# Moving the split of the next unit's values, the maxima ahead of it and the row scales in a fused attention and feed-forward kernel

## The chip, the cores and the metric

The kernel runs on one core of one Trainium2 chip. The metric is the device time of one execution in microseconds. The kernel before takes 1301.77 us (median of three runs, 1301.55 to 1302.38).

## What is computed

Eight batches with eight heads each, 576 tokens, head dimension 64. The scores of a head are thresholded: a row keeps only the scores within `tau` of its maximum, takes their softmax, and multiplies it with the values. The heads of a batch are put side by side (512 columns), and the 4608 rows go through a feed-forward layer with 2048 hidden columns and softplus between its two products.

```python
scores = scale * np.matmul(q, k.transpose(0, 1, 3, 2))
thresh = np.max(scores, axis=-1, keepdims=True) - tau
scores = np.where(scores >= thresh, scores, -1000000000.0)
attn = np.exp(scores - np.max(scores, axis=-1, keepdims=True))
attn = attn / (np.sum(attn, axis=-1, keepdims=True) + 1e-09)
x = np.matmul(attn, v)                       # then heads side by side
h = x @ w_in
out = (np.maximum(h, 0.0) + np.log1p(np.exp(-np.abs(h)))) @ w_out
```

## The kernel before

**Units, tiles and steps.** A unit is a pair of heads of one batch: 32 units. Each has nine tiles of 128 rows of scores by 576 columns (tile 4 holds the last 64 rows of both heads). The outer loop (L1020) runs over all 288 tiles; its pass for tile `t` of unit `u` is called step `t` of unit `u` here. A step does the parts of several tiles at once, in an order that a string of letters gives (`PAT`, L35: `RemhlTfpSxfvwp`). In the step of tile g these are:

- R: `row_max` (L493) of tile g+2, on DVE, written to `negm`.
- e: `exps` (L499) of tile g+2, on ACT: the exponentials `e_all`, and a small operation that makes the threshold `thr`.
- m: `mask` (L504) of tile g+1, on DVE: compares the scores in PSUM with `thr` and multiplies `e_all`, summing the row into `sums`. It is the last reader of the tile's scores.
- h: `weights_hi` (L569) of tile g+1, on POOL: the upper 16-bit half `h` of the weights.
- l: `weights_lo` (L578) of tile g, on DVE: the lower half, also called `h` in the profile. It needs POOL's half of the same tile, made a step earlier.
- T: `weights_T` (L583) of tile g-1: a transposing DMA of both halves, on SP's queue, to `eT`.
- f (twice): a share of the feed-forward products on PE (`h` L725, `o` L789). Their share of each step is set by hand (`Q9`, L40). Softplus (`st`, on ACT) and its halves (`g`, on POOL) and the additions (`acc`, on DVE) follow.
- p (twice): a point, at which deferred work becomes due (`defer`, L888: n points later).
- S: `scores` (L475) of tile g+3, on PE. There are two PSUM buffers for scores, so those of tile g+3 take the one that the mask of tile g+1 has freed.
- x: `extras` (L948): everything that comes once a unit.

**The order on the engines.** From step 36 on, every operation on DVE, ACT and POOL is tied behind the one that was issued before it on the same engine (class `Queue`, L149), so these three run in the order of the program text. PE and SP have no such tie: their order is fixed when the program is built, by the order of the text and by what is expected to be ready. [...] What the three tied engines run is recorded under line 156.

**What comes once a unit.** In `extras` of unit `u`: products of weights and values (`values`, L595, steps 7 and 8 of the same unit and 2 and 3 of the next, nine matmuls `pv` each, then an ACT copy and a DVE addition to `xp`); splitting and transposing keys and queries of the next unit (steps 0 to 8, L936); loads of keys and queries of the unit after (steps 7 and 8). The values of unit `u+1` are handled in unit `u`: `load_v` (L366, three DMAs to `vn`, one buffer) at step 0, `top_v` (L376) at step 3, `split_v` (L393) at step 7. `top_v` takes the maxima of `vn` on DVE (`vtop`); two points later PE spreads them over the partitions, one point later DVE makes the power of two `v_scale` of them. `split_v` scales `vn` on ACT in place, one point later POOL writes its 16-bit halves to `vt` (two buffers), and four points later `turn_v` (L399) copies them with swapped partitions by two DMAs. This concerns units 5 to 31; the first five (`whole`, L341) use unsplit weights and values.

**Row scales.** `row_scales` (L616) adds 1e-9 to the row sums, multiplies by `v_scale` and takes the reciprocal, two DVE operations on 128 by 9 numbers (`rs`). `extras` calls it at step 8. At step 1 of the next unit (`RT`, L39) `row_scales_T` has PE transpose them; ACT, a DMA out and three DMAs back spread them to `R`, and seven points later POOL multiplies `xp` by `R`. The result, halved by `split_x` (L698), is the input of the feed-forward layer, which works in chunks: six of its main chunks (512 rows, one batch) begin at steps 43, 80, 116, 152, 188 and 224 (L910), so one takes four units.

```python
  if t == RT and prev:
      row_scales_T(prev)
  if t == 8:
      row_scales(cur)
...
  else:
      times = ((s.i - 1, 0), (s.i - 1, 3), (s.i - 1, 7))
  for at_, f in zip(times, (load_v, top_v, split_v)):
      plan.setdefault(at_, []).append(lambda f=f, s=s: f(s))
```

Of the kernel before, what the change touches and what calls it, by code (L numbers as in the profile page):

```python
# [38 lines left out]
RT = 1  # L39
# [26 lines left out]
def tile_kernel(ctx: ExitStack, tc: tile.TileContext, q, k, v, tau, w_in, w_out, out):  # L66
# [270 lines left out]
    for b in range(B):  # L337
        for hp in range(NPAIR):
            s = Unit()
# [243 lines left out]
    def weights_T(s, t):  # L583
        if t in (0, M):
            j = int(t == M)
            s.eT[j] = apool.tile([P, 9, S], F16, tag="eT", bufs=2, name=f"eT_{s.i}_{j}")
        h = s.e16.pop(t)
        if t == M:
            for j in range(2):
                nc.sync.dma_start_transpose(s.eT[j][:, :, SM:S], h[j * SR:(j + 1) * SR])  # L590
            return
        j, c = divmod(t, NC + 1)
        nc.sync.dma_start_transpose(s.eT[j][:, :, c * P:(c + 1) * P], h)

    def values(s, g):  # L595
        if g == 0:
            s.xp = apool.tile([P, S], F32, tag="xp", bufs=NX, name=f"xp_{s.i}")
        j, x0 = g // 2, g % 2 * HS
        o = ps_g.tile([P, 512], F32, tag="g", name=f"pv_{s.i}_{g}")

        steps = [(v_slot(j, NC), NC)]
        for c in range(NC):
            steps += [(v_slot(j, c), c), (10 + v_slot(j, c), 2 * NC - c)]
        for n, (a, b) in enumerate(steps):
            nc.tensor.matmul(o[:, 0:HS], s.vt[:, a, :], s.eT[j][:, b, x0:x0 + HS], start=(n == 0), stop=(n == 2 * NC))  # L605
        defer(1, lambda: values_out(s, g, o))
# [9 lines left out]
    def row_scales(s):  # L616
        s.rs = apool.tile([P, 9], F32, tag="rs", name=f"rs_{s.i}")
        if s.whole:
            vec.tensor_scalar(out=s.rs, in0=s.sums, scalar1=1e-9, scalar2=None, op0=ALU.add)
        else:  # L620
            vec.tensor_scalar(out=s.rs, in0=s.sums, scalar1=1e-9, scalar2=v_scale[:, s.i:s.i + 1],
                              op0=ALU.add, op1=ALU.mult)
        vec.reciprocal(s.rs, s.rs)

    def row_scales_T(s):
        ps = ps_g.tile([P, 512], F32, tag="g", name=f"rT_{s.i}")
        nc.tensor.transpose(ps[0:9, 0:P], s.rs, ident)
        defer(1, lambda: row_scales_out(s, ps))
# [307 lines left out]
    def pre(s, first_):  # L936

        def a():
            split_k(s)
        def b():  # L940
            split_q(s, 0)
            qkT(s, 0, 0)
        def d():
            split_q(s, 1)
        return [a, b, lambda: qkT(s, 0, 2), lambda: qkT(s, 0, 1), d, lambda: qkT(s, 1, 0), lambda: qkT(s, 1, 1),
                lambda: qkT(s, 1, 2)]

    def extras(i, t):  # L948

        cur = units[i]  # L950
        nxt = units[i + 1] if i + 1 < len(units) else None
        prev = units[i - 1] if i else None
        for s, t_ in ((prev, t + 9), (cur, t)):
            if s and t_ in (VW if s.whole else VO):
                (whole_values if s.whole else values)(s, (VW if s.whole else VO).index(t_))
        if t == RT and prev:
            row_scales_T(prev)
        if t == 8:
            row_scales(cur)
        if nxt:  # L960
            if t == 0:
                cur.nxt = pre(nxt, False)
            for n, f in enumerate(cur.nxt):
                if ST[n] == t:
                    f()
        for f in plan.pop((i, t), ()):
            f()
        for at_, f in zip(LD, (load_k, load_q)):
            if t == at_ and i + 2 < len(units):
                f(units[i + 2])  # L970

    plan = {}
    for s in units:
        if s.i == 0:
            times = ((0, -1), (0, 0))
        elif s.i == 1:
            times = ((0, -1), (0, 4))
        elif s.whole:
            times = ((s.i - 1, 4), (s.i - 1, 7))
        else:  # L980
            times = ((s.i - 1, 0), (s.i - 1, 3), (s.i - 1, 7))
        for at_, f in zip(times, (load_v, top_v, split_v)):
            plan.setdefault(at_, []).append(lambda f=f, s=s: f(s))

# [35 lines left out]
    for g, (cur, t) in enumerate(tiles):  # L1020
# [7 lines left out]
        for step in PAT:  # L1028
# [6 lines left out]
            elif step == "h" and nxt and not nxt[0].whole:  # L1035
                weights_hi(*nxt)
            elif step == "l" and not cur.whole:
                weights_lo(cur, t)
            elif step == "R" and ahead:
                row_max(*ahead)  # L1040
            elif step == "e" and ahead:
                exps(*ahead)
            elif step == "m" and nxt:
                mask(*nxt)
            elif step == "f":
                upto += quota / PAT.count("f")
                while done < upto:
                    done += next(ffn)
            elif step == "x":
                extras(cur.i, t)  # L1050
            elif step == "S" and g + 3 < NS:
                scores(*tiles[g + 3])
            elif step == "v":
                slow_products()
            elif step == "w":
                while prep and prep[0][0] <= g:
                    _, f, a = prep.pop(0)
                    f(*a)
            elif step == "p":
                point()  # L1060

    last = units[-1]
    weights_T(*tiles[-1])
    rest = {15: lambda: row_scales_T(last), 21: lambda: values(last, 2), 24: lambda: values(last, 3)}
    for n, _ in enumerate(ffn):
# [35 lines left out]
```

## Time and profile before

| | us |
|---|---|
| median of three runs | 1301.77 |
| the profiled execution, its own time | 1300.2 |
| its span, first to last instruction | 1298.4 |
| PE busy | 1231.9 |
| DVE busy | 931.2 |
| POOL busy | 912.7 |
| ACT busy | 906.2 |

A row of a group or of the timeline names the start (timeline only), the busy time, the engine, the line, the operation, what it writes and reads (`out<-in`), the shape and the count; in brackets stands the time that the engine was idle before it and what ended that. PEld is TensorE's loading of weights, which overlaps its products. A row of waits gives who waited for whom, the total in us, the number of times and the longest. In the timeline, instructions of one kind that follow one another are merged into one row. In the window that the next section uses, 665 to 674 us, the masks (`e_all<-s,thr,e_all`) of 666.04, 668.93 and 672.97 us belong to step 7 and step 8 of unit 18 and step 0 of unit 19; the steps of units 8 to 24 take 573 us, from 296 to 869 us.

### The profile page before, as it was taken

The numbers are of one execution on the slowest core, as the hardware profiler recorded it, in microseconds if no ns is written. First come the engines' busy times: TensorE is split into PE (matmuls) and PEld (weight loads), VectorE is DVE, ScalarE is ACT, GpSimd is POOL, SyncE is SP. The second block draws the span as 40 slices with busy tenths as digits, with TensorE's granted clock in tenths as the row PEclk, the third lists the DMA queues.
The fourth block names the chain that finished last, engine by engine and source line by source line (L and its number), as shares of the span: only waits on it lengthen the run. The fifth ranks groups of instructions, "written<-read, shape, count | busy, mean of one in ns | idle before, by whom it ended". The sixth has DMA issues, their size and how long they took to land.

```text
span 1298.4 us, 21573 instructions
## 1 busy us (share of the span) xinstructions
PE 1231.9 (95%) x7045; PEld 741.9 (57%) x7045; DVE 931.2 (72%) x1738; ACT 906.2 (70%) x1715; POOL 912.7 (70%) x986
## 2 busy tenths in 40 slices
PE   6988987898999999999999999999999999999998
PEld 5655544454566566556555655665657755554455
DVE  6878888989878887788778977786677666640111
ACT  5877887877777777777777787778676767744321
POOL 2577788978876787778776886688667777564332
PEclk9999999999999999999999999999999999999999
DMA  4544458865877788778777787787667665520010
GB/s 130 161 140 125 129 131 166 174 123 122 174 146 147 144 168 163 151 144 175 144 148 144 168 148 148 145 153 147 129 128 162 115 132 106 101 66 17 1 42 17
DMA packets 368737, 167.90 MB, mean 129 GB/s; under 512 B 320208, under 2 KB 346224, under 8 KB 368624
## 3 DMA queue, kind: packets, MB, share of 16 engines
q1 hardware_dynamic: 368624, 166.52, 61.6%
q8 instruction: 56, 0.92, 0.3%
q14 instruction: 57, 0.47, 0.1%
HBM read 56.62 MB, written 10.63 MB: 52 GB/s over the span
## 4 chain that ended last, share of the span: by engine, by line
PE 42%; ACT 17%; DVE 15%; POOL 13%; issue 8%; DMA 4%; SPq 0%; POOLq 0%; DVEq 0%; ACTq 0%
PE o L789 14%; PE h L725 14%; PE s L490 7%; ACT st L156 5%; ACT L156 5%; POOL g L156 4%; DVE e_all L156 3%; DVE h L156 3%; PE pv L605 3%; DVE negm L156 3%; ACT e_all L156 2%; PE pv L559 2%; POOL xl L156 2%; DMA eT<-h 2%; POOL h L156 2%
## 5 line engine op out<-in xcount | busy, mean ns | idle before, releaser
L789 PE MATMUL o<-w_o,g 128*128 128x512 f16 x1728 | 407.1, 381 | 3.3 <-DVE xp L156 1.5
L725 PE MATMUL h<-xh,w_i 128*128 128x512 f16 (+1 forms) x1280 | 361.3, 359 | 4.5 <-ACT kT L156 2.0
L156 POOL TENSOR_SCALAR h<-e_all 128x576 f16<-128x576 f32 x243 | 228.5, 943 | 112.6 <-DVE e_all L156 110.3
L156 ACT ACTIVATE e_all<-s,negm 128x576 f32<-128x576 f32 x288 | 213.6, 742 | 116.6 <-DVE negm L156 110.5
L725 PEld LDWEIGHTS <-w_i 128*128 128x128 f16 x1920 | 179.9, 98 | 168.8 <-issue 11.7
L156 DVE SCALAR_TENSOR_TENSOR e_all<-s,thr,e_all 128x576 f32<-128x576 f32 x288 | 232.8, 809 | 48.9 <-ACT thr L156 48.8
L156 DVE TENSOR_REDUCE negm<-s 128x1 f32<-128x576 f32 x288 | 214.9, 746 | 66.5 <-PE s L490 64.8
L789 PEld LDWEIGHTS <-g 128*128 128x128 f16 x1728 | 159.7, 98 | 176.4 <-issue 7.0
L156 DVE SCALAR_TENSOR_TENSOR h<-e_all,h 128x576 f16<-128x576 f32 x243 | 236.4, 973 | 20.2 <-POOL h L156 19.6
L725 PE MATMUL h<-xl,w_i 128*128 128x512 f16 (+1 forms) x640 | 230.2, 360 | 1.4 <-POOL xl L156 1.3
L156 POOL TENSOR_SCALAR g<-st 128x512 f16<-128x512 f32 x144 | 97.8, 679 | 164.6 <-ACT st L156 162.4
L156 DVE SCALAR_TENSOR_TENSOR acc<-o,c,acc 128x512 f32<-128x512 f32 x108 | 80.1, 743 | 154.5 <-PE o L789 154.1
L156 POOL TENSOR_TENSOR g<-st,g 128x512 f16<-128x512 f32 x144 | 171.9, 1194 | 12.0
L490 PE MATMUL s<-kT,q 128*128 128x288 f32 x768 | 152.7, 328 | 19.3 <-DVE e_all L156 16.7
L156 ACT ACT_TABLE_LOAD x119 | 152.7, 1283 | 4.1 <-DVE negm L156 1.9
L490 PEld LDWEIGHTS s<-kT,q 128*128 128x128 f32 x768 | 114.7, 192 | 57.1 <-DVE e_all L156 44.7
L605 PE MATMUL pv<-eT,vt 128*128 128x288 f16 x972 | 140.6, 288 | 3.9 <-DVE xp L156 2.4
L156 ACT ACTIVATE st<-h,c 128x512 f32<-128x512 f32 x144 | 91.0, 683 | 76.3 <-PE h L725 75.5
L490 PE MATMUL s<-kT,qT 128*128 128x288 f32 x512 | 106.2, 329 | 10.1 <-DVE e_all L156 9.8
L605 PEld LDWEIGHTS <-vt 128*128 128x128 f16 x972 | 89.3, 98 | 38.1 <-issue 5.3
L156 ACT COPY xp<-pv 64x288 f32<-64x288 f32 (+3 forms) x133 | 50.5, 384 | 78.3 <-PE pv L605 74.1
L156 ACT ACTIVATE st<-st,c 128x512 f32<-128x512 f32 x144 | 96.2, 715 | 2.3
(112 smaller groups left out, 1513.8 us busy)
## 6 DMA issues: line engine op xcount, KB each, us to landing
q<-q SPq DMA_DIRECT2D x62, 192.0 KB
kn<-in_k_dram SPq DMA_DIRECT2D x32, 256.0 KB
qn<-in_q_dram SPq DMA_DIRECT2D x32, 256.0 KB
vn<-in_v_dram SPq DMA_DIRECT2D x32, 256.0 KB
wc_i<-in_moe_w_in_dram SPq DMA_DIRECT2D x16, 512.0 KB
wc_o<-in_moe_w_out_dram SPq DMA_DIRECT2D x16, 512.0 KB
qT<-qT SPq DMA_DIRECT2D x62, 128.0 KB
out_dram<-acc SPq DMA_DIRECT2D x14, 512.0 KB
```

What stands on the lines that cost most here:

```text
L156: i = getattr(self.eng, name)(*args, **kwargs)
L490: nc.tensor.matmul(sp[:, hf, 0:HS], lhs, s.kT[j][:, hf * HS:(hf + 1) * HS], start=(m == 0), stop=(m == len(parts) - 1))
L559: nc.tensor.matmul(o[0:D, 0:n], s.vn[k_, v_slot(j, c), :], h[k_, c, 0:n], start=(c == 0), stop=(c == NC))
L605: nc.tensor.matmul(o[:, 0:HS], s.vt[:, a, :], s.eT[j][:, b, x0:x0 + HS], start=(n == 0), stop=(n == 2 * NC))
L725: nc.tensor.matmul(bank[:, i * u.T:(i + 1) * u.T], wi[g, cc][:, a, e], x[cc], start=(cc == 0 and m == 0), stop=(cc == NCC - 1 and m == 2))
L789: nc.tensor.matmul(o, u.g[fc][m // 2][:, sl], wo[fc][:, m % 2, :], start=(n == 0), stop=(n == 3 * QF - 1))
```

## The change

Three things move. The maxima of the next unit's values are taken at step 2 instead of step 3, and the values are split at step 5 instead of step 7 (units 5 to 31). The row scales of a unit are made at step 0 of the next unit instead of step 8 of its own, for all units; for the last one, which has no next, after the loop.

```diff
-        if t == 8:
-            row_scales(cur)
+        if t == RT - 1 and prev:
+            row_scales(prev)
...
-            times = ((s.i - 1, 0), (s.i - 1, 3), (s.i - 1, 7))
+            times = ((s.i - 1, 0), (s.i - 1, 2), (s.i - 1, 5))
...
     last = units[-1]
+    row_scales(last)
     weights_T(*tiles[-1])
```

## The prediction

> **What bounds the kernel now.** First the page, for the engines' shares.
>
> ```profile
> PE 1231.9 (95%) x7045; PEld 741.9 (57%) x7045; DVE 931.2 (72%) x1738; ACT 906.2 (70%) x1715; POOL 912.7 (70%) x986
> ```
>
> TensorE is busy for 95% of 1298.4 us, and none of the steps that the change moves is work of TensorE except one small transposition. So the time can move only by what TensorE waits, and the change has to be read through the other engines' queues. The table by stretch shows where those waits can be.
>
> ```profile
> 166.00:296.00 130.00, 110.43 (x586) 62.84 (x586) 116.73 (x209) 108.34 (x198) 109.66 (x106) 0.96 0.69 145
> 296.00:869.00 573.00, 561.39 (x3285) 342.17 (x3284) 471.93 (x867) 427.34 (x784) 441.01 (x480) 1.00 0.78 152
> 869.00:1112.00 243.00, 239.29 (x1456) 150.15 (x1455) 162.93 (x308) 180.12 (x313) 177.56 (x194) 1.00 0.66 132
> ```
>
> The columns are stretch, length, then busy time of PE, PEld, DVE, ACT and POOL. The middle stretch holds units 8 to 24, 17 of the 27 units whose values are split. There PE idles 573.00 - 561.39 = 11.6 us. In the last (units 25 to 30) the idle time is 3.7 us and DVE is busy for only 163 of 243 us, so there is room for moved work. In the first (units 5 to 7) every engine is over 83% busy, weights being prepared there too. The list of waits, asked for the middle stretch, says what TensorE waits for.
>
> ```profile
> PEld s L490 <- DVE e_all L156: 28.3, 70, 1.1
> DVE negm L156 <- PE s L490: 27.8, 40, 1.0
> DVE e_all L156 <- ACT thr L156: 26.2, 29, 1.9
> ...
> PE s L490 <- DVE e_all L156: 5.4, 13, 0.6
> ```
>
> The scores (L490) of a tile need the PSUM buffer that the mask (`e_all` on DVE, L506) of the tile two before frees. That is the one wait that counts, and 13 times it reaches PE itself; the mask in turn waits for ScalarE's `thr`. The timeline shows where. These are steps 7 and 8 of unit 18 on PE and its weight loads.
>
> ```profile
> 665.47 1.27 PE L605 MATMUL pv<-eT,vt 128*128 128x288 f16 x9
> 666.57 0.38 PE L789 MATMUL o<-w_o,g 128*128 128x512 f16 x1
> 666.92 0.79 PE L490 MATMUL s<-kT,q 128*128 128x288 f32 x4
> 667.56 1.90 PE L789 MATMUL o<-w_o,g 128*128 128x512 f16 x8
> 669.79 0.80 PE L490 MATMUL s<-kT,q 128*128 128x288 f32 x4 [0.33 <-DVE e_all L156]
> ```
> ```profile
> 669.79 0.57 PEld L490 LDWEIGHTS s<-kT,q 128*128 128x128 f32 x4 [0.83 <-DVE e_all L156]
> ```
>
> Scores of step 8 start at 669.79, 0.33 us late on PE. Those of step 7 (666.92) stand behind nine `pv` and one `o`, which the source puts after them (letter S ahead of x): PE's order is not written by hand like the other three, and work was drawn ahead where scores were not expected to be ready. This decides the price below. On DVE the same moments are these.
>
> ```profile
> 666.04 0.82 DVE L156 SCALAR_TENSOR_TENSOR e_all<-s,thr,e_all 128x576 f32<-128x576 f32 x1 [0.69 <-ACT thr L156]
> 666.78 0.08 DVE L156 DVE_READ_ACCUMULATOR e_all<-s,thr,e_all 128x1 f32 x1
> 667.13 1.21 DVE L156 SCALAR_TENSOR_TENSOR h<-e_all,h 128x576 f16<-128x576 f32 x1 [0.26 <-POOL h L156]
> 668.26 0.74 DVE L156 TENSOR_REDUCE negm<-s 128x1 f32<-128x576 f32 x1
> 668.93 0.80 DVE L156 SCALAR_TENSOR_TENSOR e_all<-s,thr,e_all 128x576 f32<-128x576 f32 x1
> ```
>
> The chain into that wait is: mask of step 7, late for ScalarE; `h` (the low halves, L580), late for POOL's `h`; then `negm`; then the mask of step 8, ending 669.73, and the scores at 669.79. ScalarE and POOL, not DVE's own load, are what is late at steps 5 to 8.
>
> **The change part by part.** *Splitting the values at step 5 instead of step 7* (`split_v`). One ScalarE operation, two on POOL, two DMAs. Where POOL does it now:
>
> ```profile
> 665.30 1.16 POOL L156 TENSOR_TENSOR g<-st,g 128x512 f16<-128x512 f32 x1
> 666.42 1.31 POOL L156 TENSOR_SCALAR h<-e_all 128x576 f16<-128x576 f32 x2
> 668.20 0.72 POOL L156 TENSOR_SCALAR vt<-vn 128x640 f16<-128x640 f32 x1 [0.47 <-ACT vn L156]
> 669.00 1.41 POOL L156 TENSOR_TENSOR vt<-vn,vt 128x640 f16<-128x640 f32 x1
> 670.38 1.18 POOL L156 TENSOR_SCALAR h<-e_all 128x576 f16<-128x576 f32 x1
> ```
>
> The pair takes 670.38 - 668.20 = 2.18 us. Deferred by one point from step 5 it is queued behind the `g` halves of that step's softplus and ahead of the two `h` at 666.42. The `g` rows run without a gap into the `h` rows, so there is no hole for it: both `h` come 2.18 us later. DVE's low halves already wait 0.26 us for the first of them, so they, `negm` and the mask of step 8 come 2.18 us later, and so may the scores. ScalarE first:
>
> ```profile
> 663.21 0.56 ACT L156 CAST kT<-tr 128x512 fp32r<-128x512 f32 x1
> 663.79 1.28 ACT L156 ACT_TABLE_LOAD   x1
> 665.09 0.74 ACT L156 ACTIVATE e_all<-s,negm 128x576 f32<-128x576 f32 x1
> ...
> 667.29 0.83 ACT L156 ACTIVATE vn<-vn,v_scale 128x640 f32<-128x640 f32 x1
> ```
>
> The 0.83 us of `vn` go ahead of `kT` at 663.21; `kT`, the table load and `e_all` follow one another without a gap, so `thr` and the mask of step 7 come 0.83 us later. This lies inside the 2.18 us and is not added to it.
>
> How much of 2.18 us reaches the end? From above: all of it. From below: nothing, if PE is given other work. I take the one row that shows such work drawn ahead: nine `pv` (666.57 - 665.47 = 1.10 us) and one `o`, (1.90 - 0.38) / 7 = 0.22 us. Behind step 8's scores stand nine `pv` again, so 1.32 us can be filled; further `o` need a PSUM buffer that DVE frees only after the late mask. That leaves 2.18 - 1.32 = 0.86 us a unit. The value lies nearer the middle because both ends need PE's order to be perfect or unchanged.
>
> In the units where a chunk ends (8, 12, 16, 20, 24) there is slack. Unit 16, step 8, on DVE and PE:
>
> ```profile
> 600.11 0.81 DVE L156 SCALAR_TENSOR_TENSOR e_all<-s,thr,e_all 128x576 f32<-128x576 f32 x1
> ```
> ```profile
> 601.50 0.88 PE L490 MATMUL s<-kT,q 128*128 128x288 f32 x4
> ```
>
> The mask ends at 600.92, the scores start 0.58 us later. 2.18 - 0.58 - 1.32 = 0.28 us a unit.
>
> The two `turn_v` DMAs now enter SP's queue at step 7 instead of the next unit's step 0. SP then waits for POOL's `vt` there, with the transposition of `h` behind it, which itself comes late for the same cause: I take nothing, at most the same 2.18 us once more hidden in the first.
>
> *Row scales at the next unit's step 0.* Two DVE operations leave the place between steps 8 and 0:
>
> ```profile
> 671.97 0.22 DVE L156 TENSOR_SCALAR rs<-sums,v_scale 128x9 f32<-128x9 f32 x1
> 672.22 0.22 DVE L156 RECIPROCAL rs<-rs 128x9 f32<-128x9 f32 x1
> 672.35 0.70 DVE L156 TENSOR_REDUCE negm<-s 128x1 f32<-128x576 f32 x1
> ```
>
> They cost 672.35 - 671.97 = 0.38 us, and advance the mask of step 0 by that; at step 1 the same 0.38 us are back. With the split gone from there, DVE's `h` is also shorter:
>
> ```profile
> 669.66 1.36 DVE L156 SCALAR_TENSOR_TENSOR h<-e_all,h 128x576 f16<-128x576 f32 x1
> ...
> 673.70 0.76 DVE L156 SCALAR_TENSOR_TENSOR h<-e_all,h 128x576 f16<-128x576 f32 x1
> ```
>
> 1.36 us beside the second `vt`, 0.76 us beside POOL's `h`: 0.60 us. Together 0.98 us of DVE ahead of step 0's scores, which however are hardly late once step 8's were; of the 28.3 / 70 = 0.40 us that a wait there averages I give back a quarter, 0.1 us a unit. The units of whole values move only the row scales: nothing. After the last unit the pair stands ahead of the closing projections: 0.38 us hidden by them, and 0.38 us if not.
>
> *Maxima at step 2 instead of step 3.* DVE, steps 2 to 3 of unit 18:
>
> ```profile
> 647.77 0.76 DVE L156 TENSOR_REDUCE negm<-s 128x1 f32<-128x576 f32 x1 [0.85 <-PE s L490]
> ...
> 650.46 0.82 DVE L156 TENSOR_REDUCE vtop<-vn 128x1 f32<-128x640 f32 x1
> ```
>
> The 0.82 us fit the 0.85 us that DVE waits for scores in the new place: nothing; without that cover 0.82 us. The values must have landed by then:
>
> ```profile
> 641.00 1.36 SPq L373 DMA_DIRECT2D vn<-in_v_dram  x2
> ```
>
> They are issued by 642.36, over 4 us before the new place (about 647). Nothing.
>
> **Sum.** Units 9-11, 13-15, 17-19, 21-23: 12 x (0.86 - 0.1) = 9.1 us. Units with a chunk's end: 5 x 0.28 = 1.4 us. Units 25 to 30: nothing (DVE has a third of the stretch free). Units 5 to 7: queues are full wherever the split stands; nothing, give or take 3 us. Together +10.5 us. The profiled execution took 1300.2 us (span 1298.4), the median of the runs is 1301.77, so 1.6 us higher; carried over, 1301.8 + 10.5 = 1312 us.
>
> **The rivals.** *Full price* (0.12): PE keeps its order and waits out everything: 12 x 2.18 + 5 x (2.18 - 0.58) = 34 us, 1336 us. For it: step 8's scores do wait now, so nothing was drawn ahead of them. Against: step 7's were given ten matmuls.
>
> *Full cover* (0.14): behind the `pv`, four further `o` (0.88 us) find a buffer, and 1.10 + 5 x 0.22 = 2.20 us fill the delay: 1302 us, no change. Against: a bank must come free while DVE stands still.
>
> *Faster* (0.21): what counts is not POOL's queue but DVE's slowness beside the split. DVE loses 0.60 us to it in the very stretch, step 7 to step 1, where its rows have no gaps. If POOL's late `h` cost nothing, because PE's new order hides them, the 0.98 us that DVE gains remove the step 8 and step 0 waits: 12 x 0.83 = 10 us at most, 1292 us. It decides if the low halves at step 7 start less than about 0.8 us later than now. Against: the rows show POOL without a hole ahead of them. [...]
>
> *The forecast* has the remaining 0.53, with a range of its own of 1304 to 1326 us: from the cover nearly full to two thirds of the full price.
>
> **How the numbers follow.** A measurement of this kernel tells about 0.2% (2.6 us) from no change. Slower: 0.53 + 0.12 = 0.65; within: 0.14; faster: 0.21. The range of 1297 to 1330 us leaves out about half of the faster case (0.11) and most of the full price (0.09).
>
> **What would show it.** Right: in units 17 to 19 `vt` on POOL directly behind the last `g`, DVE's `h` of step 7 waiting about 2 us for POOL's `h`, scores of step 8 behind a run of `pv` and `o`, the unit's period up by about 0.6 us (10.5 / 17) from 573.00 / 17 = 33.7; `vtop` without a wait for its load; DVE's `h` of step 8 near 0.8 us. Wrong: PE's waits for `e_all` at most 28 us in the middle stretch, a period of 33.7 us or less, or a difference that comes from units 5 to 7 or 25 to 30.

## The result and the profile after

The changed kernel takes 1341.01 us (median of four runs, 1340.75 to 1345.18) against 1301.66 us of the kernel before, timed beside it. The ratio is 1.03, with a 95% interval of 1.0282 to 1.0319: 39 us slower. The forecast was slower, but 1312 us, and 1341 lies outside its range. The profiled execution is the slowest of the four; its span is 1343.4 us.

The page of the kernel after has almost the same work in it, and PE is busy 13.5 us longer without an instruction more:

```profile
PE 1245.4 (93%) x7045; PEld 746.4 (56%) x7045; DVE 927.4 (69%) x1738; ACT 906.0 (67%) x1715; POOL 910.1 (68%) x986
```

The same three stretches (units 5 to 7, 8 to 24, 25 to 30), again cut at the masks of their first tiles; columns as in the prediction, then granted clock, DMA share and GB/s:

```profile
173.30:306.20 132.90, 109.27 (x577) 62.10 (x578) 115.91 (x209) 109.01 (x199) 110.65 (x107) 0.97 0.69 144
306.20:916.00 609.80, 573.72 (x3295) 346.72 (x3293) 467.98 (x867) 427.43 (x783) 440.75 (x479) 0.98 0.72 143
916.00:1158.00 242.00, 237.90 (x1451) 149.47 (x1450) 162.07 (x308) 179.32 (x311) 173.98 (x194) 1.00 0.66 131
```

Units 8 to 24 take 609.8 us instead of 573.0. These 36.8 us are most of the 45.0 us between the two profiled executions (1343.4 - 1298.4; the medians differ by 39). They are of two kinds. PE's idle time there is 609.80 - 573.72 = 36.1 us, against 11.6 before: 24.5 us more. And PE's busy time is 573.72 against 561.39: 12.3 us more for the same matmuls, with a granted clock of 0.98 where it was 1.00. Units 5 to 7 lose 2.9 us here (6.7 in the profile of the split alone, the first experiment below), units 25 to 30 nothing (242.0 against 243.0). Units 0 to 4 take 7.3 us more in this one execution, but 1.9 us more in the profile of that experiment, which has the same split. Most of the difference is clock: three stretches at half the granted clock, 17.1 us together, against two with 6.8 us before, by estimate (17.1 - 6.8) / 2 = 5.1 us. I do not count it as a cost of the change.

The list of waits in units 8 to 24 names the idle time:

```profile
PEld s L490 <- DVE e_all L156: 44.1, 49, 2.2
...
DVE h L156 <- POOL h L156: 34.4, 25, 1.8
...
PE s L490 <- DVE e_all L156: 27.3, 17, 1.9
```

PE's wait for the mask is 27.3 us in 17 waits, 16 of them at step 8, where it was 5.4; these 21.9 us are nearly all of the new idle time. DVE's `h` waits 34.4 us for POOL's `h`. Before, it waited 9.7:

```profile
DVE h L156 <- POOL h L156: 9.7, 19, 0.8
```

The timelines of steps 5 to 8 of unit 18 show the chain, POOL first:

```profile
696.40 1.16 POOL L156 TENSOR_TENSOR g<-st,g 128x512 f16<-128x512 f32 x1
697.52 0.72 POOL L156 TENSOR_SCALAR vt<-vn 128x640 f16<-128x640 f32 x1
698.33 1.40 POOL L156 TENSOR_TENSOR vt<-vn,vt 128x640 f16<-128x640 f32 x1
699.70 1.30 POOL L156 TENSOR_SCALAR h<-e_all 128x576 f16<-128x576 f32 x2
```
```profile
697.76 0.82 DVE L156 SCALAR_TENSOR_TENSOR e_all<-s,thr,e_all 128x576 f32<-128x576 f32 x1 [1.42 <-ACT thr L156]
700.40 1.20 DVE L156 SCALAR_TENSOR_TENSOR h<-e_all,h 128x576 f16<-128x576 f32 x1 [1.82 <-POOL h L156]
701.53 0.74 DVE L156 TENSOR_REDUCE negm<-s 128x1 f32<-128x576 f32 x1
702.20 0.80 DVE L156 SCALAR_TENSOR_TENSOR e_all<-s,thr,e_all 128x576 f32<-128x576 f32 x1
702.93 0.75 DVE L156 SCALAR_TENSOR_TENSOR h<-e_all,h 128x576 f16<-128x576 f32 x1
```

The pair `vt` stands directly behind the last `g`, both upper halves come 2.18 us later (699.70 - 697.52), DVE's low half waits 1.82 us for the first of them, and `negm` and the mask of step 8 follow late. PE and its queue at the same place:

```profile
694.49 2.12 PE L789 MATMUL o<-w_o,g 128*128 128x512 f16 x9
696.44 1.27 PE L605 MATMUL pv<-eT,vt 128*128 128x288 f16 x9
697.54 1.03 PE L789 MATMUL o<-w_o,g 128*128 128x512 f16 x4
698.64 0.79 PE L490 MATMUL s<-kT,q 128*128 128x288 f32 x4
699.27 1.25 PE L789 MATMUL o<-w_o,g 128*128 128x512 f16 x5
700.36 0.78 PE L605 MATMUL pv<-eT,vt 128*128 128x288 f16 x5
703.07 0.79 PE L490 MATMUL s<-kT,q 128*128 128x288 f32 x4 [1.93 <-DVE e_all L156]
...
704.27 2.55 PE L789 MATMUL o<-w_o,g 128*128 128x512 f16 x11
```

Before, the order was nine `pv`, one `o`, scores of step 7, eight `o`, scores of step 8, nine `pv`. Now three of the eight `o` have gone ahead of step 7's scores, so that many fewer stand ahead of step 8's scores, and five of the nine `pv` have gone ahead of those. They wait 1.93 us on PE where they waited 0.33. In the units where a chunk ends the order on PE did not change at all: in unit 16, PE does nine `o`, five `pv`, scores, four `pv`, four `o`, five `h` before and after, and the last row shows the wait in the place of none.

```profile
627.12 0.79 PE L490 MATMUL s<-kT,q 128*128 128x288 f32 x4
627.76 0.67 PE L605 MATMUL pv<-eT,vt 128*128 128x288 f16 x4
628.26 1.03 PE L789 MATMUL o<-w_o,g 128*128 128x512 f16 x4
...
631.35 0.79 PE L490 MATMUL s<-kT,q 128*128 128x288 f32 x4 [0.98 <-DVE e_all L156]
```

**The clock.** The other 12.3 us are matmuls that ran slowly. Behind the wait at step 8 of unit 9 (1.87 us), the same 11 `o` take 4.24 us instead of 2.55:

```profile
379.17 0.79 PE L490 MATMUL s<-kT,q 128*128 128x288 f32 x4 [1.87 <-DVE e_all L156]
...
380.37 4.24 PE L789 MATMUL o<-w_o,g 128*128 128x512 f16 x11
```

The granted clock was 0.5 from 380.41 on for 3.41 us. Units 9 to 24 have six such stretches (at 380.4, 452.1, 523.8, 561.3, 738.8 and 882.2 us); the kernel before has none there. (A seventh, at 305.3 us, reaches 2.5 us into unit 8.) Counted from 380.41, the other five start 21, 42, 53, 105 and 147 times 3.413 us later (452.09 - 380.41 = 21 x 3.413), so in this trace they lie on one grid. Cut along that grid, the trace gives pairs of neighbouring windows; the first column behind the comma is PE's busy time, the granted clock stands third from the end:

```profile
701.27:704.68 3.41, 1.61 (x11) 1.23 (x12) 3.41 (x8) 1.20 (x3) 1.12 (x1) 1.00 0.74 159
704.68:708.09 3.41, 3.41 (x19) 1.86 (x18) 3.38 (x9) 1.25 (x4) 1.82 (x3) 1.00 1.04 220
735.40:738.81 3.41, 1.47 (x11) 0.98 (x10) 3.32 (x6) 0.92 (x2) 1.32 (x3) 1.00 0.74 162
738.81:742.23 3.42, 3.42 (x13) 1.57 (x12) 3.41 (x7) 1.48 (x4) 1.45 (x2) 0.50 1.10 196
```

A window in which PE idled 3.41 - 1.61 = 1.80 us is followed by full clock, one with 1.94 us idle by half clock. In units 9 to 24, all six half-clock windows follow a window with 1.87 to 1.94 us idle, and no window with 1.80 us or less is followed by one. The waits of the twelve ordinary units (those without a chunk's end) are alike (1.87 to 1.94 us); six of them fall into one window of the grid, and half clock follows each of these; the other six straddle two, and none is followed by it. Each such window costs about 1.7 us (4.24 - 2.55), six of them 10 us, and the part of the seventh about 1.2 us, half of its length. In this stretch 1.87 us of idle time in one window (377.00 to 380.41 us) were enough.

### The profile page after: what moved, and what is told of

It reads as the page before. It is cut to its first block, busy times and chain, and to the rows that moved or that the text cites. A ratio compares the mean times of both kernels' runs of the same rounds, so it can differ in the third digit from the quotient of the medians.

```text
span 1343.4 us, 21575 instructions
## 1 busy us (share of the span) xinstructions
PE 1245.4 (93%) x7045; PEld 746.4 (56%) x7045; DVE 927.4 (69%) x1738; ACT 906.0 (67%) x1715; POOL 910.1 (68%) x986
## 4 chain that ended last, share of the span: by engine, by line
PE 40%; ACT 19%; POOL 18%; DVE 10%; issue 9%; DMA 3%; SPq 1%; POOLq 0%; DVEq 0%; ACTq 0%
PE h L725 13%; PE o L789 13%; PE s L490 7%; ACT st L156 6%; ACT L156 6%; POOL g L156 6%; PE pv L605 3%; DVE negm L156 3%; ACT e_all L156 3%; DVE e_all L156 3%; POOL h L156 2%; POOL xl L156 2%; POOL vt L156 2%; PE pv L559 2%; POOL xp L156 1%
## 5 line engine op out<-in xcount | busy, mean ns | idle before, releaser
L789 PE MATMUL o<-w_o,g 128*128 128x512 f16 x1728 | 415.0, 387 | 2.8 <-DVE xp L156 1.3
L156 DVE SCALAR_TENSOR_TENSOR h<-e_all,h 128x576 f16<-128x576 f32 x243 | 230.0, 947 | 47.7 <-POOL h L156 47.7
L490 PE MATMUL s<-kT,q 128*128 128x288 f32 x768 | 155.4, 332 | 45.5 <-DVE e_all L156 42.4
L605 PE MATMUL pv<-eT,vt 128*128 128x288 f16 x972 | 144.8, 291 | 8.4 <-ACT qT L156 2.9
```

What stands on the lines that cost most here:

```text
L156: i = getattr(self.eng, name)(*args, **kwargs)
L490: nc.tensor.matmul(sp[:, hf, 0:HS], lhs, s.kT[j][:, hf * HS:(hf + 1) * HS], start=(m == 0), stop=(m == len(parts) - 1))
L789: nc.tensor.matmul(o, u.g[fc][m // 2][:, sl], wo[fc][:, m % 2, :], start=(n == 0), stop=(n == 3 * QF - 1))
```

## The experiments

Each experiment is timed against the kernel before on the same chip; that one took 1302.0 to 1302.5 us. The theory: two POOL operations ahead of the upper halves make the mask of step 8 late, and PE waits. Rivals: the maxima or the row scales do it, ScalarE's part of the split does it, the two moved DMAs do it, or PE's order does it and could be mended by hand.

**Which part: the split alone, the maxima alone, the row scales alone, and both without the split.**

```diff
-        times = ((s.i - 1, 0), (s.i - 1, 3), (s.i - 1, 7))
+        times = ((s.i - 1, 0), (s.i - 1, 3), (s.i - 1, 5))   # split alone
+        times = ((s.i - 1, 0), (s.i - 1, 2), (s.i - 1, 7))   # maxima alone
```

The row scales alone are the other two hunks of the change; the fourth kernel is the changed one with the split back at step 7.

> Only the split moves, to step 5; maxima and row scales stay. Theory A (POOL's queue): the split alone delays POOL's halves, with them DVE's low halves and the mask of step 8; it carries the whole loss, 1335 to 1345 us. Rival B (DVE's queue: row scales and maxima now stand in the stretch where DVE has no gaps, and they share the loss): at most half of it, 1310 to 1325 us.

> Only the maxima move, to step 2. Theory A: hidden in DVE's wait for scores, 1299 to 1304 us. Rival B: 0.82 us more on DVE ahead of step 3's mask in each of 27 units, up to 15 us, 1306 to 1317 us.

> Only the row scales move, to the next unit's step 0. Theory A: 0.38 us of DVE change places where no scores are late, 1299 to 1304 us. Rival B: slower, 1306 us or more, since step 1's mask gets them.

> Maxima and row scales move, the split stays at step 7. Theory A: 1298 to 1304 us, near the kernel before. Rival B: slower by the greater part of 39 us, 1320 us or more.

Split alone: 1342.15 us, ratio 1.0312 (1.0298 to 1.0326). Maxima alone: 1304.33 us, 1.0021 (1.0009 to 1.0033). Row scales alone: 1300.83 us, 0.9993 (0.9982 to 1.0004). Both without the split: 1304.52 us, 1.0026 (1.0014 to 1.0038). The split carries the whole loss. The row scales cost nothing. The maxima were expected to cost nothing and cost 1 to 4 us. The waits in units 8 to 24, of the kernel before and then of the one with the maxima moved, suggest where:

```profile
PE topv L382 <- DVE xp L156: 1.2, 1, 1.2
```
```profile
PE topv L382 <- DVE xp L156: 4.6, 4, 1.2
```

Moved one step, the spreading of the maxima on PE (`topv`) stands, in units 9, 13, 17 and 21 (each the first after a chunk's end), ahead of the time when DVE's `xp` frees the PSUM buffer it needs. PE waits there 3.4 us more than before, and units 8 to 24 take 575.9 us instead of 572.8, 3.1 more (here and below cut at the masks to 0.1 us; 573.0 was cut at whole microseconds). PE's wait for the mask hardly grew (5.9 us against 5.4), so DVE's 0.82 us, on which the prediction looked, are nearly hidden; the wait is that of the matmul that follows two points later. No run moved `topv` by itself.

**Which operation of the split: ScalarE's, POOL's or the DMAs.** The changed kernel with POOL's halves and the DMAs back at their old place, ScalarE's scaling still at step 5:

```diff
-        defer(1, lambda: halves(s.vt[:, 0:10, 0:D], s.vt[:, 0:10, D:2 * D], s.vn))
-        defer(4, lambda: turn_v(s))
+        defer(5, lambda: halves(s.vt[:, 0:10, 0:D], s.vt[:, 0:10, D:2 * D], s.vn))
+        defer(8, lambda: turn_v(s))
```

> The changed kernel, with POOL's two halves and the two copies of the values back at step 7; only ScalarE's scaling of the values stays at step 5. Theory A (POOL's queue carries the loss): ScalarE's 0.83 us make the mask of step 7 late, and DVE's low halves by about 0.65 us after it; 1303 to 1313 us. Rival C (ScalarE's queue at steps 5 to 7 carries it): 1325 us or more.

1303.76 us, 1.0006 (0.9993 to 1.0020): no difference from before, with the maxima and the row scales moved as in the change. ScalarE's 0.83 us cost nothing. What costs is POOL's two operations or the DMAs, which the next run separates. The waits of units 8 to 24 agree:

```profile
DVE h L156 <- POOL h L156: 4.4, 8, 0.9
...
PE s L490 <- DVE e_all L156: 0.3, 1, 0.3
```

And with only the DMAs back at their old time (`turn_v` deferred by 8 points, the halves still early):

> The changed kernel, with the two copies of the values (the DMAs) back at their old place, POOL's two operations at step 5. Theory A: 1337 to 1345 us, as the changed kernel. Rival F (SP's queue, which the two copies block ahead of the transposition of the weights): 1325 us or less.

1342.19 us, 1.0306 (1.0292 to 1.0320). The DMAs are not it; POOL's two operations are.

**How much of the delay.** Only the first of POOL's two operations early (0.72 of 2.18 us), the second one and the DMAs at the old time:

```diff
+        defer(1, lambda: pool.tensor_scalar(out=s.vt[:, 0:10, 0:D], in0=s.vn, scalar1=1.0, scalar2=1.0, op0=ALU.mult, op1=ALU.mult))
+        defer(5, lambda: pool.tensor_tensor(out=s.vt[:, 0:10, D:2 * D], in0=s.vn, in1=s.vt[:, 0:10, 0:D], op=ALU.subtract))
+        defer(8, lambda: turn_v(s))
```

> The changed kernel, with only the first of POOL's two operations (0.8 us of 2.18) at step 5; the second and the copies are back at step 7. Theory A: the loss goes with POOL's time ahead of the weights' halves; ScalarE's lateness of about 0.65 us lies inside it, so DVE is about 0.8 us late, PE's waits stay short enough for the clock; 1305 to 1316 us. Rival E (it is all or nothing, any of the split's work on POOL at step 5 breaks PE's order): 1325 us or more.

1308.23 us, 1.0046 (1.0033 to 1.0060): 6 us, where a third of 39 us would be 13. Units 8 to 24 of it, and two of its waits there (its line numbers are shifted by one):

```profile
300.20:877.50 577.30, 560.05 (x3285) 342.56 (x3284) 467.03 (x867) 427.34 (x783) 448.20 (x479) 1.00 0.77 151
```
```profile
DVE h L156 <- POOL h L156: 9.3, 25, 0.8
PE s L491 <- DVE e_all L156: 5.5, 13, 0.5
```

PE idles 17.3 us, 5.6 more than before, its busy time is about that of before (561.4), and the clock is 1.00. The two waits are as long as before: what PE waits longer for is `topv` (4.5 us against 1.2, which comes with the maxima) and the transposition of the next keys (2.1 against 0.3).

This run, the one with POOL's halves put back and the changed kernel have the same order on PE in unit 18, with five `pv` ahead of step 8's scores. So that order does not come from POOL's delay. Leaving aside the two runs below whose order on PE was set by hand, it stands in every run with ScalarE's scaling at step 5 and in none of the others. The masks of steps 6 and 8 lie 8.04 us apart with the halves put back, 8.63 with the upper half early and 10.11 in the changed kernel, after 7.96 before: a delay of 0.08, 0.67 and 2.15 us. The scores of step 8 wait less than 0.2, 0.45 and 1.93 us, after 0.33. The five `pv` take about 0.61 us, and 0.33 + 0.67 - 0.61 = 0.39 and 0.33 + 2.15 - 0.61 = 1.87 us. A third of the delay thus costs less than a third because the five `pv` nearly cover it, and because the granted clock stayed at 1.00 there, where the changed kernel's was 0.98.

**Can PE's order fill the delay?** This is the prediction's fill term, tried by hand: at step 8 of the changed kernel the scores stand behind all of the step's own extra work and the second feed-forward share. In the kernel before they stand behind the extra work alone (`PAT8 = "RemhlTfpxSfvwp"`).

```diff
+PAT8 = "RemhlTfpxfSvwp"
-        for step in PAT:
+        for step in (PAT8 if t == 8 and not cur.whole else PAT):
```

> The changed kernel, with the scores of step 8 issued behind the values and behind the second share of feed-forward products (units of split weights). Theory A, its part on PE's order (the delay costs what it costs only because PE stands still for it): about 2 us of products fill the wait, the half-clock windows that follow such a wait go as well; 1303 to 1318 us. Rival D (the delay is handed on along DVE, so that later scores wait instead): 1330 us or more.

> The kernel before, with the scores of step 8 issued behind the values of that step. If the wait of about 0.4 us at step 8 is PE's order alone, it goes: 1295 to 1300 us. Rival: row maxima of the next step then wait for the later scores, 1302 us or more.

Both were expected to gain and both lost. On the changed kernel: 1355.45 us, 1.0409 (1.0396 to 1.0423), 14 us worse than the change. On the kernel before: 1312.60 us, 1.0077 (1.0063 to 1.0091). PE at step 8 of unit 18 in the first one, where one more line ahead shifts all line numbers by one:

```profile
700.24 1.26 PE L790 MATMUL o<-w_o,g 128*128 128x512 f16 x5
701.33 1.27 PE L606 MATMUL pv<-eT,vt 128*128 128x288 f16 x9
702.43 0.81 PE L790 MATMUL o<-w_o,g 128*128 128x512 f16 x3
705.07 0.28 PE L424 MATMUL tr<-identr,k 128*128 128x128 f32 x1 [1.82 <-DVE xp L157]
...
705.66 0.88 PE L491 MATMUL s<-kT,q 128*128 128x288 f32 x4
```

All nine `pv` and three further `o` now run while DVE is late, so they found their buffers. Then PE stops at the transposition of the next keys, which waits 1.82 us for a PSUM buffer that DVE's `xp` frees, and DVE does `xp` behind the same late mask. The wait is the old one under another name, and now the scores stand behind it: DVE's `negm` waits 53.1 us for scores in units 8 to 24, after 42.0 in the changed kernel. In the kernel before it is the same place:

```profile
674.33 1.27 PE L606 MATMUL pv<-eT,vt 128*128 128x288 f16 x9
676.48 0.28 PE L424 MATMUL tr<-identr,k 128*128 128x128 f32 x1 [0.88 <-DVE xp L157]
676.60 0.76 PE L491 MATMUL s<-kT,q 128*128 128x288 f32 x4
```

So drawing the `pv` ahead did not gain: behind them the order comes to an operation that itself waits for the late DVE. An order with other products in place of that transposition was not tried.

**One step earlier or later.** The kernel before with the split at step 6, at step 8, and the changed kernel with the maxima back at step 3 and the split at step 8 (that is, the row scales moved and the split one step later):

```diff
-        times = ((s.i - 1, 0), (s.i - 1, 3), (s.i - 1, 7))
+        times = ((s.i - 1, 0), (s.i - 1, 3), (s.i - 1, 6))
+        times = ((s.i - 1, 0), (s.i - 1, 3), (s.i - 1, 8))
```

> The kernel before, with the split at step 6. Theory A: POOL's halves of the values now stand behind the first of the two upper halves of the weights, the one that DVE waits for at step 7, and only the second is late, by about 0.3 us for DVE; nearly the whole loss is gone, 1299 to 1307 us. Rival C (any split in steps 5 and 6 collides on ScalarE): 1315 us or more.

> The kernel before, with the split at step 8. Theory A (what counts is whether POOL's halves of the values stand ahead of an upper half that DVE is about to need): behind step 8's upper half POOL waits 2.3 us for DVE in three of four units, so the 2.18 us fit; 1297 to 1304 us. Rival C (any move away from step 7 costs, by buffers or by the load that waits for them): 1310 us or more.

> The split at step 8 and the row scales at the next unit's step 0, maxima at step 3. Theory A: the two parts add, 1296 to 1303 us; a version faster than the kernel before would have to come from here. Rival C: 1310 us or more.

At step 6: 1316.71 us, 1.0115 (1.0099 to 1.0130), 14 us where at most 5 had been expected. The scores wait no longer than before there (5.2 us against 5.4 in units 8 to 24). The loss is the same mechanism one step later: `vt` now stands ahead of the upper half that DVE needs at step 8. DVE waits 0.53 us for it in each ordinary unit, where it did not wait, and 2.98 us at the end of units 12, 16, 20 and 24, where POOL also has the next chunk's `xh` and `xl` and DVE had waited 0.81. On PE the transposition of the next keys then waits for DVE's `xp`, 8.6 us where it was 0.3. In the profile, units 8 to 24 take 584.7 us instead of 572.8, 11.9 more; how much of that is clock was not taken apart (the mean granted clock of the two executions is 0.989 and 0.993). POOL and DVE at the end of unit 16:

```profile
609.54 1.16 POOL L156 TENSOR_TENSOR xl<-xp,xh 128x512 f16<-128x512 f32 x1
610.66 0.73 POOL L156 TENSOR_SCALAR vt<-vn 128x640 f16<-128x640 f32 x1
611.48 1.40 POOL L156 TENSOR_TENSOR vt<-vn,vt 128x640 f16<-128x640 f32 x1
612.85 1.31 POOL L156 TENSOR_SCALAR h<-e_all 128x576 f16<-128x576 f32 x2
```
```profile
613.55 1.21 DVE L156 SCALAR_TENSOR_TENSOR h<-e_all,h 128x576 f16<-128x576 f32 x1 [2.99 <-POOL h L156]
```

At step 8: 1298.63 us, 0.9979 (0.9969 to 0.9989). With the row scales moved as well: 1296.22 us, 0.9955 (0.9942 to 0.9969), 0.45% faster than the kernel before. POOL in unit 18 of that one:

```profile
668.61 1.12 POOL L156 TENSOR_SCALAR h<-e_all 128x576 f16<-128x576 f32 x1 [2.09 <-DVE e_all L156]
669.70 0.72 POOL L156 TENSOR_SCALAR vt<-vn 128x640 f16<-128x640 f32 x1
670.50 1.40 POOL L156 TENSOR_TENSOR vt<-vn,vt 128x640 f16<-128x640 f32 x1
671.87 1.18 POOL L156 TENSOR_SCALAR h<-e_all 128x576 f16<-128x576 f32 x1
```

Around the end of a unit POOL idles for about 2 us, waiting for the mask (2.31 us before in unit 18, behind step 8's upper half). With the split at step 8, `vt` stands behind the upper half of step 8 instead of ahead of it, and the next upper half is hardly later for it: the 2.1 us of POOL's work lie in time in which it had idled. Units 8 to 24 take 568.2 us instead of 572.8.

## Why the prediction was wrong, step by step

*What bounds it, and the chain:* right. The loss is in units 8 to 24, at the scores of step 8, by the chain that was named: `vt` ahead of POOL's `h`, DVE's low half (1.82 us of waiting), `negm`, the mask, PE. The masks of steps 6 and 8 of unit 18 lie 10.11 us apart instead of 7.96, 2.15 us more for 2.18 forecast. That the change does this was shown by the split alone and by POOL's halves put back.

*"1.32 us can be filled":* this step failed. The prediction took nine `pv` and one `o`, seen drawn ahead of step 7's scores, as what would be drawn ahead of step 8's when POOL is late. PE's order did not answer to POOL's delay: five `pv` stand ahead of those scores, and they stand there just as well when POOL's halves are put back. By the prediction's own duration they take 5/9 of 1.10 us or 0.61 us, so 2.15 - 0.61 = 1.54 us a unit remain instead of 0.86. In the twelve ordinary units PE waits 1.87 to 1.94 us, 1.6 more than the 0.33 of eight of them before (1.3 more than the 0.56 to 0.58 of the other four). The units' periods, cut at the masks of their first tiles, agree: unit 19 takes 35.08 us for 33.52, and units 18 and 22, without a half-clock window, 35.09 and 35.08 for 33.71. Over the twelve units that is 18 us at full clock instead of the 9.1 of the sum. The nine `pv` could have run earlier, as the changed kernel with the scores set behind them showed, and so could three further `o`, of which the prediction had said that they need a PSUM buffer that DVE frees too late. But PE then waited as long at the next transposition, on a buffer that DVE does free behind the late mask. Why the program's order drew exactly five ahead stays open.

*Chunk-end units, 0.28 us each:* the same step. Its 0.58 us of slack were there, but nothing at all was drawn ahead. PE waits 0.98 us in unit 16, and the period rises from 32.07 to 34.27 us. DVE's `h` there also lasts 1.15 us instead of 0.76, beside POOL's `xh`. Most of these 2.2 us belongs to the split: with the split alone the period is 34.07 us, 2.0 more, and with the maxima alone 32.82, 0.8 more, so the two do not add up. Units 12, 16, 20 and 24 lose 2.2 us each at full clock, 8.8 together; unit 8 loses nothing.

*What was missing:* the granted clock. The prediction priced waits as idle time only. Six of the twelve waits cost about 1.7 us of half-speed matmuls on top, 10 us together, a term that the sum does not have. By the units' periods 18 us (ordinary units), 8.8 us (chunk-end units) and 10 us (clock) make up the 36.8 us of the stretch, where the sum had 10.5. The clock's part is read from the traces; that it follows PE's idle time within one window of the grid is what units 9 to 24 of the changed kernel's profile show (six windows, 1.87 to 1.94 us idle), but no experiment moved a wait against the grid on purpose.

*Maxima at no cost:* wrong by 1 to 4 us. Only the moved DVE operation was priced and not the matmul that follows it, whose waits are of that size. *Row scales, DMAs, ScalarE's part, units 25 to 30 at nothing:* right. *Units 5 to 7, nothing give or take 3 us:* 2.9 us more, inside the margin, but 6.7 in the profile of the split alone; what sets this was not taken apart.

*The rivals.* "Full price" comes nearest (1336 us), in part by accident: PE did not wait out all of 2.18 us, but the clock added 10 us where the five `pv` saved 12 x 0.61 = 7.3. "Faster" named a real thing: DVE's `h` at step 8 fell from 1.36 to 0.75 us once `vt` had gone. In the new place `vt` (697.52 to 699.73) met no `h` of DVE's in unit 18, because DVE was at the mask and then stood waiting for POOL. So these 0.61 us were saved. They gained nothing, because what delayed the scores lay ahead of that `h`.

## What to carry to other kernels

The price of a step that is moved is not its own duration but what stands behind it on each queue, and who waits for that; look for the place where that engine is idle anyway, and put it there. When a delay is set off against work that could be drawn ahead, count only what stands ahead in the order that will run, and ask of the piece behind it which buffer it needs and whether the late engine is the one that frees it; where that can't be shown free, count the delay in full. Where TensorE is the bound, look in the trace also for what follows a wait: here six waits of 1.87 to 1.94 us, each within one window of 3.41 us, were followed by half the granted clock and cost about 1.7 us on top in the matmuls behind them (4.24 - 2.55), and six of 1.88 to 1.94 us across two windows were not.

## What the runs showed of the hardware

A single wait of 1.9 us, in a stretch in which TensorE is 94% busy (573.7 of 609.8 us), was followed by half the granted clock for 3.41 us. This was not expected, nor that the switch is so sharp in units 9 to 24. There, in the changed kernel's profile, windows of the grid with at most 1.80 us idle kept the full clock (the most that did), and those with at least 1.87 us lost it (the least that did); the ends of matmuls in the profile are modelled. Elsewhere it is not so clean: in the same profile a window with 1.54 us idle (from 69.80 us) lost the clock, and one with 1.73 us (from 264.36 us) kept it; why is open. A wait of the same length that straddles two windows cost little but itself: behind one of 1.88 us (to 810.73 us; 0.58 before) the clock stayed at 1.00, and the period of unit 22 rose by 1.37 us, from 33.71 to 35.08, where that of unit 10, with a half-clock window, rose from 33.71 to 36.76.
